# Attention and gated MLP on one core: transpositions in two tiles of 64 rows with split loads, the first pair's features written in place, and an order drawn anew

## The chip, the cores and the metric

The kernel runs on one core of a Trainium2 chip. The metric is the device time of one execution in microseconds; for the kernel before, the median of three runs is 740.95 us (740.59 to 742.3). Engines are named as in the profile: PE (TensorE matmul), PEld (its weight loads), DVE (VectorE), ACT (ScalarE), POOL (GpSimd) and SP, whose queue issues nearly all DMAs.

## What is computed

```python
# q, k, v: (4, 8, 768, 64); proj: (64, 6)
q_bits = einsum('bhsd,dk->bhsk', q, proj) > 0        # the same for k
mask = q_bucket[:, :, :, None] == k_bucket[:, :, None, :]
scores = where(mask, q @ k.T / 8, -1e9)
attn_out = softmax(scores) @ v                       # per batch and head
x = attn_out.transpose(0, 2, 1, 3).reshape(4, 768, 512)
h = gelu(x @ w_in); u, v = h[..., :512], h[..., 512:]
v_n = layernorm(v) * g_ln
v_s = einsum('ts,bsd->btd', w_sg, v_n) + b_sg[None, :, None]
out = x + (u * v_s) @ w_out
```

## The kernel before

The attention works on 16 pairs of heads (`NPAIR`), two heads side by side on the 128 partitions, 64 rows each. For each pair:

- `load` brings q and k in, one DMA per head and operand (4 per pair, all on SP's queue), as 128 token rows in partitions, 6 tiles of tokens, 2 x 64 columns. One buffer each holds q and k, so the next pair's load waits until the last reader of this pair's is done.
- `parts` transposes each with six 128x128 float32 transpositions (line L526; the identity streams, the data are the weights). ACT copies the result back into the same buffer (L536). `high` (ACT, L530) and `low` (DVE, L533) split it in a rounded part and a rest (`hq`, `lq`, `hk`, `lk`).
- `features` multiplies with the projection `pw`, 32 columns wide, four products side by side in four column tiles of the array (L553). `sign` (DVE, L556) makes bit features `fc` of it, and `scatter` sends them with four DMAs on SP's queue to their rows in `fq` and `fk` (L569). These were set to zero at the start by POOL (L486).
- `largest` ("M" below): for each of 6 tiles of queries and 2 halves of keys, four matmuls of 64 rows (two heads at once in two row tiles, feature product plus score product, L584) into two PSUM banks, and DVE takes the largest (L589, tile `mx`).
- `shift` spreads the maxima into a feature row (DVE L597, PE L602, ACT L608).
- `weigh` ("W"): for each of 12 tiles, eight matmuls of 64 rows (L624), ACT's exponential to `p` (L629), POOL's sums (L642).
- `weighted` ("AV"): the products with v (L654), for each half of the queries; the sums over keys (L678), and for the pair two ahead the feature products. `finish` sends the sums through DRAM and back as a reciprocal (SP: L695, L696, L699, L701; DVE: L697), scales the result on DVE (L703, `xt`) and stores it (L705).

PSUM has eight banks; an M and a W take two each. Maxima run four steps (`AHEAD`) ahead of the W that they belong to. Beside the attention the weights of the MLP are converted in jobs on DVE, POOL and ACT (L372 to L392). The MLP that follows (L845 hidden v, L876 hidden u, L894 gate, L923 output; four batches) streams dense matmuls; the first batch's hidden v starts inside the attention's end.

The order of all this is not the code's order. `Plan.add` takes for each step an engine, a cost and a priority; `Plan.order` runs a list scheduler over them and records instructions in that order, and each engine takes its own in order. The numbers at the top of the file (`HID`, `AVP`, `PREP`, `OM`, ...) are offsets of those priorities.

Of the kernel before, what the change touches and what calls it, by code (L numbers as in the profile page):

```python
# [21 lines left out]
MLP = {"xl": "POOL", "gm": "DVE", "gl": "POOL", "wg": 450.84, "wo": 131.34, "x": 480}  # L22
# [3 lines left out]
HID = 308.55  # L26
AVP = 3.07
S0P = -1.32
AHEAD = 4
PREP, SHIFTP, FINP, WSTEP, WP = 8.92, -3.65, 6.26, 37.69, 29.58  # L30
LOADS = "SP"
GPLACE = 4
XLATE = 7.75
FEAT = 2.17
LOWP = 7.32
LOADP = -0.4
LATF = 3.2
# [11 lines left out]
ADDW = 1  # L49


class Plan:
# [23 lines left out]
    def __init__(self):  # L76
        self.groups, self.tags = [], {}
# [21 lines left out]
    def add(self, engine, cost, prio, fn, r=(), w=(), dma=0, port=None, form=None, lat=0.0):  # L99

        port = engine == "POOL" if port is None else port
        g = {"e": engine, "c": cost, "p": prio, "fn": fn, "dma": dma, "n": len(self.groups), "slots": [], "port": port, "form": form, "lat": lat}
# [163 lines left out]
def kernel(  # L266
# [58 lines left out]
    frow = setup.tile([1, 2, P], F32, name="frow")  # L325
    nc.vector.memset(frow, 0.0)
    fv = frow.rearrange("a f (s b c) -> a f s b c", s=2, c=FB)
# [6 lines left out]
    nc.vector.memset(fv[:, 1, 1, :, MROW:MROW + 1], 1.0)  # L334
    pw = const.tile([P, 2, Q], F32, name="pw")
# [13 lines left out]
    fcol = const.tile([P, 2], F32, name="fcol")  # L349
# [88 lines left out]
    for i in range(2):  # L438
        nc.tensor.transpose(psb[:, 7, i:i + 1], frow[:, i, :], ident[:1, :1])
    nc.vector.tensor_copy(fcol, psb[:, 7, 0:2])  # L440
# [16 lines left out]
    if True:  # L457
# [27 lines left out]
        for t in ftiles[0] + ftiles[1]:  # L485
            nc.gpsimd.memset(t.bitcast(F32), 0.0)  # L486
# [15 lines left out]
        def load(n, prio):  # L502
# [3 lines left out]
            for s, (nm, src) in enumerate((("q", q), ("k", k))):  # L506
                t = early.ring([P, NT, 2, D], F32, nm, 1)
                for j in range(2):
                    def fn(eng, t=t, j=j, src=src):
                        eng.dma_start(t()[:, :, j, :], src[st.b, 2 * st.hp + j].rearrange("(t p) d -> p t d", t=NT))  # L510
                    dma(prio + 0.2 * s, 1.09, fn, w=[(t, j)], e=LOADS)
# [7 lines left out]
        def parts(st, s, prio):  # L519
# [3 lines left out]
            def tr():  # L523
                for hf in range(2):
                    for i in range(HT):
                        nc.tensor.transpose(tp()[:, hf, i * P:(i + 1) * P],  # L526
                                            raw()[:, hf * HT + i].rearrange("p j d -> p (j d)"), ident)
# [7 lines left out]
            plan.add(PE, 0.654, prio, tr, [raw], [tp])  # L535
            plan.add(ACT, 0.81, prio, lambda: nc.scalar.copy(x_of(raw).rearrange("p (a b) -> p a b", a=2), tp()[:, :, :SH]), [tp], [raw])  # L536
            def split(p1, p2):
                plan.add(ACT, 0.81, p1 + OH[s], high, [raw], [hh])
                plan.add(DVE, 0.98, p2 + OL[s], low, [raw, hh], [lo], port=True)
# [6 lines left out]
        def features(st, prio, merged=False):  # L546
# [13 lines left out]
            else:  # L560
                plan.add(PE, 0.66, prio, project, st.raw, [fp], form="col32")
            st.sign = lambda prio: plan.add(DVE, 0.56, prio, sign, [fp], [fc])
            st.fc = fc

# [8 lines left out]
        def largest(st, t, prio):  # L573
# [13 lines left out]
            for kh in range(2):  # L587
                plan.add(PE, 0.346, prio + 0.01 * kh + OM[2 * t + kh], lambda kh=kh: mm(kh), [*st.hi, *st.ft], [sc[kh]], form="row")
                plan.add(DVE, 0.95, prio + OM[2 * t + kh], lambda kh=kh: nc.vector.tensor_reduce(  # L589
                    mx()[:, i, :, kh], sc[kh]()[:, :, :SH], axis=AX.X, op=ALU.max, negate=True), [sc[kh]], [(mx, (kh, i))])  # L590

        def shift(st, hf, prio):
# [5 lines left out]
                m()[:, :, MROW::BL], mx(), axis=AX.X, op=ALU.min), [mx], [m])  # L598
# [5 lines left out]
            plan.add(PE, 0.18, prio, spread, [m], [tp])  # L604
# [381 lines left out]
```

## Time and profile before

| | us |
|---|---|
| median of 3 runs | 740.95 |
| the profiled execution's own time | 739.75 |
| its span, first to last instruction | 738.0 |
| PE busy in the span | 717.1 |
| DVE busy | 544.0 |
| POOL busy | 459.8 |
| ACT busy | 379.5 |

The span has a start (to about 30 us, when PE waits for loads and features), the attention (to 434 us), a passage in which the attention's last halves are finished beside the first batch's MLP, and from there to the end the MLP. Busy PE time counts overlapping and pipelined matmuls as one stretch; it tells where PE waits, and how fast it streams is read from start times.

### The profile page before, as it was taken

The page shows a single profiled execution, that of the slowest core. Times are in us where ns is not written, and L with a number is a line of the kernel's source. Part 1 is how long each engine was busy: PE and PEld are TensorE (multiplying, and loading weights), DVE is VectorE, ACT ScalarE, POOL GpSimd, SP SyncE. Part 2 cuts the span into 40 slices and gives each one's busy share as a digit, 9 for nine tenths or more (in the row PEclk, how much of TensorE's full clock was granted, in tenths as well). Part 3 has the DMA queues.
Part 4 walks back from the last instruction along what each step waited for, and adds up shares of the span by engine and source line. Part 5 has one row for each costly group of instructions (what it writes and reads, how often), then busy time and mean ns, then how long its engine had stood idle before and what let it go on. Part 6 is the DMA issues. An engine that isn't in the chain of part 4 may idle for free.

```text
span 738.0 us, 14443 instructions
## 1 busy us (share of the span) xinstructions
PE 717.1 (97%) x5300; PEld 566.5 (77%) x5300; DVE 544.0 (74%) x859; ACT 379.5 (51%) x623; POOL 459.8 (62%) x465
## 2 busy tenths in 40 slices
PE   6899999999999999999999999999999999999997
PEld 5676676666767666676766669998999889988996
DVE  3887899788898888878788878655864486347733
ACT  3565566665757656565765556530761066106510
POOL 2578889889887878778597976570463045404230
PEclk8999999999999999999999999999999999999999
DMA  6214543653675464255343235935220601061004
GB/s 139 70 45 103 127 114 90 154 132 94 155 143 123 93 149 108 70 128 125 96 108 95 73 85 135 239 68 139 34 64 23 157 15 43 1 147 25 1 1 115
DMA packets 180839, 70.59 MB, mean 96 GB/s; under 512 B 158112, under 2 KB 170528, under 8 KB 180768
## 3 DMA queue, kind: packets, MB, share of 16 engines
q1 hardware_dynamic: 180320, 69.01, 39.3%
q10 hardware_dynamic: 448, 0.66, 0.6%
q8 instruction: 42, 0.69, 0.4%
q14 instruction: 29, 0.24, 0.1%
HBM read 51.61 MB, written 17.24 MB: 93 GB/s over the span
## 4 chain that ended last, share of the span: by engine, by line
PE 76%; DMA 10%; DVE 9%; SPq 2%; issue 2%; ACT 1%; POOL 0%; DVEq 0%; ACTq 0%
PE psb L624 15%; PE psb L654 13%; PE psb L894 11%; PE psb L923 9%; PE psb L845 8%; PE psb L876 7%; PE psb L584 7%; DVE mx L589 4%; DMA r<-sq 2%; PE psb L526 2%; DMA rs<-r 2%; PE psb L678 1%; PE psb L553 1%; DMA sq<-s 1%; PE psb L602 1%
## 5 line engine op out<-in xcount | busy, mean ns | idle before, releaser
L642 POOL TENSOR_TENSOR sum<-sum,p 128x384 f32<-128x384 f32 x256 | 240.7, 977 | 54.8 <-ACT p L629 54.7
L589 DVE TENSOR_REDUCE mx<-psb 128x2 f32<-128x768 f32 x192 | 174.2, 950 | 39.7 <-PE psb L584 39.2
L629 ACT ACTIVATE p<-psb 128x768 f32<-128x768 f32 x192 | 147.1, 815 | 24.3 <-PE psb L624 20.8
L654 PE MATMUL psb<-p,v 128*64 128x385 f32 x768 | 131.2, 491 | 0.0
L654 PEld LDWEIGHTS psb<-p,v 128*64 128x64 f32 x768 | 52.3, 137 | 71.7 <-issue 62.4
L642 POOL TENSOR_TENSOR sum<-p,p 128x384 f32<-128x384 f32 x64 | 71.2, 1133 | 19.5 <-ACT p L629 19.5
L624 PE MATMUL psb<-hq,hk 64*128 64x384 f32 x384 | 72.0, 370 | 5.3 <-DVE mx L589 5.1
L584 PE MATMUL psb<-fk,fq 64*128 64x384 f32 x384 | 68.8, 353 | 2.3 <-DVE mx L589 2.3
L855 POOL TENSOR_TENSOR mv<-mv,epsr 128x1 f32<-128x1 f32 x24 | 13.8, 574 | 86.4 <-DVE mv L854 81.2
L584 PE MATMUL psb<-hk,hq 64*128 64x384 f32 x384 | 66.0, 339 | 0.0
L624 PE MATMUL psb<-lq,hk 64*128 64x384 f32 x384 | 64.9, 333 | 0.0
L624 PE MATMUL psb<-fq,fk 64*128 64x384 f32 x384 | 64.9, 332 | 0.0
L624 PE MATMUL psb<-hq,lk 64*128 64x384 f32 x384 | 64.8, 332 | 0.0
L894 PE MATMUL psb<-wgl,zh 128*128 128x384 f32 x192 | 64.2, 335 | 0.4 <-POOL wgl L817 0.4
L894 PE MATMUL psb<-wgh,zh 128*128 128x384 f32 x192 | 64.1, 334 | 0.0
L894 PE MATMUL psb<-wgh,zl 128*128 128x384 f32 x192 | 64.1, 334 | 0.0
L905 POOL TENSOR_TENSOR gs<-gt,gs 128x384 fp32r<-128x384 f32 x32 | 33.6, 1056 | 48.9 <-ACT gs L902 45.6
L669 ACT COPY un<-psb 128x385 f32<-128x385 f32 x32 | 15.4, 482 | 94.1 <-PE psb L654 94.1
L829 ACT ACTIVATE h<-psb 128x384 f32<-128x384 f32 (+1 forms) x56 | 29.4, 535 | 66.8 <-PE psb L845 59.9
L923 PE MATMUL psb<-woh,gs 128*128 128x512 f32 x192 | 59.9, 389 | 0.0
L897 DVE TENSOR_TENSOR gt<-psb,b_bc 128x384 f32<-128x384 f32 x32 | 17.8, 556 | 46.3 <-PE psb L894 43.5
L624 PEld LDWEIGHTS psb<-hq,hk 64*128 64x128 f32 x384 | 36.1, 184 | 16.8 <-DVE mx L589 11.3
(111 smaller groups left out, 1576.4 us busy)
## 6 DMA issues: line engine op xcount, KB each, us to landing
q<-in_q_dram SPq DMA_DIRECT2D x32, 192.0 KB, 4.3
k<-in_k_dram SPq DMA_DIRECT2D x32, 192.0 KB, 3.6
v<-in_v_dram SPq DMA_DIRECT2D x16, 384.0 KB
rs<-r SPq DMA_DIRECT2D x64, 96.0 KB, 3.0
xs<-xt SPq DMA_DIRECT2D x32, 192.0 KB, 3.3
x<-xs SPq DMA_DIRECT2D x16, 384.0 KB, 3.5
rx<-xs SPq DMA_DIRECT2D x96, 64.0 KB, 2.3
out_dram<-ob SPq DMA_DIRECT2D x24, 256.0 KB, 2.3
```

The source lines that it names most:

```text
L584: nc.tensor.matmul(sc[kh]()[:, j, :SH], x[0]()[row(j), qs], x[1]()[row(j), kh * SH:(kh + 1) * SH], start=(n == 0), stop=(n == 1))
L589: plan.add(DVE, 0.95, prio + OM[2 * t + kh], lambda kh=kh: nc.vector.tensor_reduce(mx()[:, i, :, kh], sc[kh]()[:, :, :SH], axis=AX.X, op=A ...
L624: nc.tensor.matmul(sc[i]()[:, j, :SH], x()[row(j), ks], y()[row(j), cs], start=(n == 0), stop=(n == 3))
L629: plan.add(ACT, 0.81, prio, lambda i=i: nc.scalar.activation(p[i]()[:, :, :SH], sc[i]()[:, :, :SH], AF.Exp), [sc[i]], [p[i], ticks[-1]])
L642: plan.add(POOL, 1.03, prio + 0.6, lambda i=i, j=j, first=first: nc.gpsimd.tensor_add(sums()[:, j], (first or sums)()[:, j, :SH], p[i]()[: ...
L654: nc.tensor.matmul(av()[row(j), :SH + 1], v_()[:, j, kt, :], p[kt]()[:, j, :], start=(kt == 0), stop=(kt == NT - 1))
L829: plan.add(ACT, ua - 0.02, prio, lambda: nc.scalar.activation(h2()[:, :n], ps()[:, :n], AF.Square), [ps], [h2])
L845: nc.tensor.matmul(ps(), x()[:, ts_], w[:, c, FH:FF], start=(c == 0 and n == 0), stop=(c == NC - 1 and n == 2))
L876: nc.tensor.matmul(ps()[:, :SH], w[:, c, fs], x()[:, cs], start=(c == 0 and n == 0), stop=(c == NC - 1 and n == 2))
L894: nc.tensor.matmul(vp()[:, :SH], z()[:, t, fs], w()[:, t, cs], start=(t == 0 and n == 0), stop=(t == NT - 1 and n == 2))
L905: nc.gpsimd if e == POOL else nc.vector).tensor_sub(gl()[:, cs], gt(), gh()[:, cs].bitcast(F32)),
L923: nc.tensor.matmul(po(), a()[:, ts_], w()[:, f, :], start=(f == 0 and n == 0), stop=(f == NF - 1 and n == 2))
```

## The change

1. **Transpositions.** For all pairs but the first, each load is split in two DMAs of 64 partitions: rows 0 to 63 hold tokens 0 to 383, rows 64 to 127 tokens 384 to 767. Each 128x128 transposition becomes two of 64 rows and 64 streamed columns, in the two row tiles of the array and into different PSUM banks. The matmuls M and W have the same two row tiles.
2. **First pair.** Its q and k keep the whole transpositions. Its features are made by `direct`: a projection `pwd` as wide as the array, whose columns lie where the features belong, for each operand and half of the tokens; DVE's sign writes straight into `fq` and `fk`. The four scatter DMAs and the zeroing of these two tiles fall away; PE has four full-width products in place of four side by side, DVE four signs in place of one. M now waits for the halves that it reads alone. One of the first pair's two k loads is issued by ACT's queue.
3. **Order.** The constants at the top are other numbers, and a table `SHAPE` adds an offset to the priority of each kind of step, cyclically by its count.

```diff
-MLP = {..., "wg": 450.84, "wo": 131.34, "x": 480}
+MLP = {..., "wg": 452.33, "wo": -53.82, "x": 459.7}
-HID = 308.55
+HID = 277.71
...
+SHAPE = {"A": [0.0, 0.0, 0.0, -1.0, ...], ..., "T": [0.03, 1.6], ...}
...
+        if tag in SHAPE:
+            i = self.count[tag] = self.count.get(tag, -1) + 1
+            prio += SHAPE[tag][i % len(SHAPE[tag])]
...
+    nc.vector.tensor_copy(pwd.rearrange("p s (i w) -> p s i w", w=FW)[:, :, :, 0], pw)
...
-        for t in ftiles[0] + ftiles[1]:
+        for t in ftiles[1]:
             nc.gpsimd.memset(t.bitcast(F32), 0.0)
...
+                    if not n:
...
+                        dma(prio + 0.2 * s, 1.09, fn, w=[(t, j)], e=ACT if s and j else LOADS)
+                    for r in range(2 if n else 0):
+                        def fn(eng, t=t, j=j, r=r, src=src):
+                            eng.dma_start(t()[row(r), :, j, :],
+                                          src[st.b, 2 * st.hp + j, r * SH:(r + 1) * SH].rearrange("(t c) d -> c t d", c=D))
+                        dma(prio + 0.2 * s, 0.55, fn, w=[(t, (j, r))], e=LOADS)
...
+                for t in range(NT):
+                    for r in range(2):
+                        nc.tensor.transpose(tp()[:, r, t * D:(t + 1) * D],
+                                            raw()[row(r), t].rearrange("p j d -> p (j d)"), ident[row(r), row(r)])
...
+        def direct(st, s, prio):
+            fp, ft = ps_two(), st.ft[s]
+            def project(hf):
+                nc.tensor.matmul(fp()[:, hf, :SH], pwd[:, s, :], x_of(st.raw[s])[:, hf * SH:(hf + 1) * SH], start=True, stop=True)
+            def sign(hf):
+                nc.vector.tensor_scalar(ft()[:, hf * SH:(hf + 1) * SH], fp()[:, hf, :SH], fcol[:, 2 + 2 * s:3 + 2 * s],
+                                        fcol[:, 3 + 2 * s:4 + 2 * s], op0=ALU.is_gt, op1=ALU.mult)
```

How the order moves is shown at three places. First PE at the third pair's transpositions, beside W (lines L624 before, L665 now) and M (L584 before, L625 now) of the pairs ahead. `hq`, `lq` and `fq` are parts and features of q, `ident` the identity. Before:

```order
L584 MATMUL psb<-fk_172,fq_171 128x384 x2
L584 MATMUL psb<-hk_0_343,hq_0_308 128x384 x2
L526 MATMUL psb<-ident,k_358 128x128 x6
L526 MATMUL psb<-ident,q_393 128x128 x6
L624 MATMUL psb<-hq_0_262,hk_0_273 128x384 x2
```

Now, on the same engine and for the same pair:

```order
L625 MATMUL psb<-hk_0_406,hq_0_364 128x384 x2
L553 MATMUL psb<-ident,q_422 128x64 x12
L665 MATMUL psb<-hq_0_271,hk_0_285 128x384 x2
L665 MATMUL psb<-hq_0_271,lk_0_303 128x384 x2
L665 MATMUL psb<-lq_0_282,hk_0_285 128x384 x2
L665 MATMUL psb<-fq_180,fk_181 128x384 x2
L625 MATMUL psb<-fk_183,fq_182 128x384 x2
L625 MATMUL psb<-hk_0_406,hq_0_364 128x384 x2
L553 MATMUL psb<-ident,k_485 128x64 x12
L665 MATMUL psb<-hq_0_271,hk_0_285 128x384 x2
```

One block of twelve full transpositions has become two blocks of twelve half ones, with a W and an M between them.

Second, PE at the start of the program (`frow` holds constants, `pw` and `pwd` the projection). Before:

```order
L526 MATMUL psb<-ident,q_249 128x128 x6
L526 MATMUL psb<-ident,k_252 128x128 x6
L553 MATMUL psb<-q_249,pw 32x384 x2
L553 MATMUL psb<-k_252,pw 32x384 x2
L526 MATMUL psb<-ident,q_285 128x128 x6
L584 MATMUL psb<-fk_170,fq_169 128x384 x2
```

Now:

```order
L548 MATMUL psb<-ident,q_258 128x128 x6
L596 MATMUL psb<-q_258,pwd 128x384
L548 MATMUL psb<-ident,k_261 128x128 x6
L596 MATMUL psb<-q_258,pwd 128x384
L596 MATMUL psb<-k_261,pwd 128x384 x2
L625 MATMUL psb<-fk_181,fq_180 128x384 x2
```

The second pair's q no longer stands ahead of the first M, and k's transpositions now stand behind the first half of q's projection.

Third, SP's queue where the thirteenth pair's q and k are loaded (`s`, `sq`, `r` and `xs` belong to `finish`). Before, the four loads:

```order
L510 DMA q_3695<-in_q_dram 128x6x64 x2
L510 DMA k_3721<-in_k_dram 128x6x64
L705 DMA xs_108<-xt_3719 128x384
L510 DMA k_3721<-in_k_dram 128x6x64
L696 DMA sq_3747<-s_0_213 128x6
```

Now:

```order
L736 DMA s_0_222<-sm_3827 4x192
L530 DMA q_3876<-in_q_dram 64x6x64 x3
L746 DMA xs_114<-xt_3892 128x384
L530 DMA q_3876<-in_q_dram 64x6x64
L530 DMA k_3920<-in_k_dram 64x6x64
L737 DMA sq_3928<-s_0_222 128x6
L530 DMA k_3920<-in_k_dram 64x6x64 x3
```

Eight issues stand where four stood, and the steps of `finish` stand among them.

## Rows read from the trace of the kernel before

**Rows 1.** Busy us by stretch: stretch, PE, PEld, DVE, ACT, POOL, then granted clock.
```profile
10.00:20.00 10.00, 6.39 (x36) 5.48 (x36) 5.39 (x7) 1.84 (x3) 0.00 (x0) 0.66 0.42 98
50.00:400.00 350.00, 342.53 (x3151) 239.99 (x3149) 300.79 (x422) 216.91 (x346) 286.54 (x293) 1.00 0.50 117
434.00:500.00 66.00, 64.87 (x342) 59.28 (x343) 46.36 (x85) 33.50 (x59) 41.06 (x33) 1.00 0.56 133
500.00:738.00 238.00, 234.25 (x1192) 213.57 (x1190) 135.72 (x249) 86.06 (x152) 75.14 (x68) 1.00 0.25 59
```

**Rows 2.** Waits, 30 to 434 us: waiting, waited for, total us, times, longest.
```profile
PE psb L624 <- DVE mx L589: 4.0, 7, 1.0
...
DVE mx L589 <- PE psb L584: 34.6, 56, 1.8
...
DVE xt L703 <- DMA rs<-r: 1.5, 2, 0.8
...
SPq L695 <- ACT sm L692: 31.1, 17, 4.1
```

**Rows 3.** Timeline of PE around one block of transpositions: start us, length us.
```profile
67.95 0.33 PE L584 MATMUL psb<-fk,fq 64*128 64x384 f32 x2
68.12 0.34 PE L584 MATMUL psb<-hk,hq 64*128 64x384 f32 x2
68.39 0.88 PE L526 MATMUL psb<-ident,k 128*128 128x128 f32 x6
69.10 0.82 PE L526 MATMUL psb<-ident,q 128*128 128x128 f32 x6
69.85 0.44 PE L624 MATMUL psb<-hq,hk 64*128 64x384 f32 x2
70.13 0.34 PE L624 MATMUL psb<-hq,lk 64*128 64x384 f32 x2
```

**Rows 4.** Groups by form: busy us, mean ns of one, idle before.
```profile
L526 PE MATMUL psb<-ident,q 128*128 128x128 f32 x96 | 14.0, 284 | 4.2 <-DMA q<-in_q_dram 3.6 <-DVE mx L589 0.6
...
L602 PE MATMUL psb<-identr,m 128*66 128x128 f32 x96 | 12.6, 240 | 0.0
...
L584 PEld LDWEIGHTS psb<-hk,hq 64*128 64x128 f32 x384 | 37.3, 189 | 0.0
...
L894 PEld LDWEIGHTS psb<-wgh,zl 128*128 128x128 f32 x192 | 36.0, 188 | 0.0
...
L526 PEld LDWEIGHTS psb<-ident,q 128*128 128x128 f32 x96 | 11.2, 145 | 5.2 <-DMA q<-in_q_dram 4.2 <-DVE mx L589 0.8
```

**Rows 5.** Chain that ended last: start us, us, what.
```profile
47.18 0.46 PE psb L678 x8
```

**Rows 6.** Timeline of the start: start us, length us, engine.
```profile
6.43 0.80 ACT L536 COPY q<-psb 128x768 f32<-128x768 f32 x1
6.75 0.85 PE L526 MATMUL psb<-ident,k 128*128 128x128 f32 x6 [0.35 <-DMA k<-in_k_dram]
8.94 0.52 PE L553 MATMUL psb<-q,pw 128*32 128x384 f32 x2 [1.34 <-ACT k L536]
9.26 0.52 PE L553 MATMUL psb<-q,pw 128*32 128x384 f32 x2
10.58 0.67 DVE L556 TENSOR_SCALAR fc<-psb,fcol 128x384 f32<-128x384 f32 x1
11.32 1.20 SPq L569 DMA_DIRECT2D fq<-fc  x2
14.81 0.69 PE L584 MATMUL psb<-fk,fq 64*128 64x384 f32 x2
15.87 5.28 DVE L589 TENSOR_REDUCE mx<-psb 128x2 f32<-128x768 f32 x6 [4.61 <-PE psb L584]
```

**Rows 7.** Issues of SP's queue by line: ns min/median/max.
```profile
L510 SPq DMA_DIRECT2D q<-in_q_dram x32: 368/532/2824, 0.7 to 368.7; - x32
...
L701 SPq DMA_DIRECT2D rs<-r x64: 444/547/1927, 63.0 to 451.5; - x64
```

More of the change, by code (lines that the diff above doesn't have):

```diff
@@ L19 @@
 DRAM = bass.MemoryType.DRAM
-MLP = {"xl": "POOL", "gm": "DVE", "gl": "POOL", "wg": 450.84, "wo": 131.34, "x": 480}
+MLP = {"xl": "POOL", "gm": "DVE", "gl": "POOL", "wg": 452.33, "wo": -53.82, "x": 459.7}
 NSUM = 3
 BANKED = False
-HID = 308.55
-AVP = 3.07
-S0P = -1.32
+HID = 277.71
+AVP = 2.95
+S0P = -1.92
 AHEAD = 4
-PREP, SHIFTP, FINP, WSTEP, WP = 8.92, -3.65, 6.26, 37.69, 29.58
+PREP, SHIFTP, FINP, WSTEP, WP = 8.63, -3.32, 2.62, 11.18, 30
 LOADS = "SP"
 GPLACE = 4
[L33 to L37, printed above, removed]
+XLATE = -0.13
+FIRST = -9.48
+FEAT = 4.51
+LOWP = 6.96
+LOADP = -3.53
+LATF = 2.6
 OM = [0.01, 0.27, 0.0, 2.44, 0.37, 0.0, -1.25, 0.68, 0.49, 1.13, -0.06, 0.0]
@@ L334 @@
     nc.vector.memset(fv[:, 1, 1, :, MROW:MROW + 1], 1.0)
+    for s in range(2):
+        for f in range(2):
+            nc.vector.tensor_copy(gv[:, s, f, :, :, 0], fv[:, f, s, :2])
+    pwd = const.tile([P, 2, P], F32, name="pwd")
+    nc.gpsimd.memset(pwd, 0.0)
     pw = const.tile([P, 2, Q], F32, name="pw")
@@ L523, in tr @@
             def tr():
[L524 to L527, printed above, removed]
+                if not st.n:
+                    for hf in range(2):
+                        for i in range(HT):
+                            nc.tensor.transpose(tp()[:, hf, i * P:(i + 1) * P],
+                                                raw()[:, hf * HT + i].rearrange("p j d -> p (j d)"), ident)
+                    return
+                for t in range(NT):
+                    for r in range(2):
+                        nc.tensor.transpose(tp()[:, r, t * D:(t + 1) * D],
+                                            raw()[row(r), t].rearrange("p j d -> p (j d)"), ident[row(r), row(r)])
             def high():
@@ L533, in low @@
                 nc.vector.scalar_tensor_tensor(lo(), x_of(raw), fac, hh().bitcast(F32), op0=ALU.mult, op1=ALU.subtract)
-            plan.add(PE, 0.654, prio, tr, [raw], [tp])
-            plan.add(ACT, 0.81, prio, lambda: nc.scalar.copy(x_of(raw).rearrange("p (a b) -> p a b", a=2), tp()[:, :, :SH]), [tp], [raw])
+            plan.add(PE, 0.35 if st.n else 0.66, prio, tr, [raw], [tp], form="row" if st.n else None, tag="T")
+            plan.add(ACT, 0.81, prio, lambda: nc.scalar.copy(x_of(raw).rearrange("p (a b) -> p a b", a=2), tp()[:, :, :SH]), [tp], [raw], tag="x")
             def split(p1, p2):
-                plan.add(ACT, 0.81, p1 + OH[s], high, [raw], [hh])
-                plan.add(DVE, 0.98, p2 + OL[s], low, [raw, hh], [lo], port=True)
+                plan.add(ACT, 0.81, p1 + OH[s], high, [raw], [hh], tag="hi")
+                plan.add(DVE, 0.98, p2 + OL[s], low, [raw, hh], [lo], port=True, tag="lo")
             st.split.append(split)
@@ L560, in features @@
             else:
[L561 to L562 removed]
+                plan.add(PE, 0.66, prio, project, st.raw, [fp], form="col32", tag="F")
+            st.sign = lambda prio: plan.add(DVE, 0.56, prio, sign, [fp], [fc], tag="sg")
             st.fc = fc
+        def direct(st, s, prio):
[5 more added lines that the diff above has]
+                                        fcol[:, 3 + 2 * s:4 + 2 * s], op0=ALU.is_gt, op1=ALU.mult)
+            for hf in range(2):
+                plan.add(PE, 0.66, prio + 0.01 * hf, lambda hf=hf: project(hf), [st.raw[s]], [(fp, hf)])
+                plan.add(DVE, 0.56, prio + 0.01 * hf, lambda hf=hf: sign(hf), [(fp, hf)], [(ft, ("f", hf))])
         def scatter(st, prio):
@@ L642, in weigh @@
                         plan.add(POOL, 1.03, prio + 0.6, lambda i=i, j=j, first=first: nc.gpsimd.tensor_add(
-                            sums()[:, j], (first or sums)()[:, j, :SH], p[i]()[:, j, :SH]), [p[i]] + ([first] if first else []), [(sums, j)])
+                            sums()[:, j], (first or sums)()[:, j, :SH], p[i]()[:, j, :SH]), [p[i]] + ([first] if first else []), [(sums, j)], tag="A")
         def weighted(st, hf, prio, owed, nxt=None):
@@ L723, in rest @@
         def rest(st, prio):
-            st.sign(prio + OF[0])
-            scatter(st, prio + OF[1])
+            if st.n:
+                st.sign(prio + OF[0])
+                scatter(st, prio + OF[1])
             for s, f in enumerate(st.split):
@@ L741 @@
             prepare(n, (-12, -3)[n])
-            features(sts[n], (-12, -3)[n] + 0.3)
+            if n:
+                features(sts[n], (-12, -3)[n] + 0.3)
+            else:
+                for s in range(2):
+                    direct(sts[n], s, FIRST + 0.1 * s)
             rest(sts[n], (-12, -3)[n] + 0.3)
```

48 lines of the change are left out of this document (25 added, 23 removed).

## The prediction

> **What bounds the kernel now.** I read the busy times by stretch first. From 50 to 400 us, the steady attention, PE is busy 342.5 of 350 us, DVE 300.8 (86%), POOL 286.5 (82%) [rows 1]. From 500 us on, the MLP, PE is busy 234 of 238 us and nothing else comes near; in the passage ahead of it 64.9 of 66. So PE is late nearly everywhere, and a microsecond of PE work taken out of the attention is worth up to a microsecond, while an order that only lets PE wait less has some 7.5 us to win in those 350.
>
> The waits come second. The longest of PE's own in the attention is W's for DVE's maxima, 4.0 us; against it DVE waits 34.6 us for M on PE [rows 2]. The two alternate, with PE ahead of DVE in need. DVE is next in line: its slack is about 14% of the time.
>
> Third, the timeline of PE around a block of transpositions. M's beats (one matmul in each of the two row tiles) start 0.17 us apart [rows 3]. The reader is to see what the block costs beyond its twelve transpositions: M's last beat starts at 68.12 and would be over for PE at 68.29; W's first starts at 69.85, and its second not 0.17 but 0.28 later. So the block takes 69.85 - 68.29 + 0.11 = 1.67 us out of PE's stream, some 0.05 of it a wait by my reading; I use 1.6. Twelve at their own pace are less: one lasts 273 ns and six 0.82 us [rows 3] (the group's mean is 284 [rows 4]), so they start (820 - 273) / 5 = 109 ns apart, 1.31 us for twelve. The other 0.3 us lies at the two edges, where PE goes from row tiles to the whole array and back.
>
> The start is a chain of its own: copy of q, transpositions and copy of k, feature products at 8.94, sign at 10.58, scatter DMAs issued from 11.32, M at 14.81, first maxima at 15.87 [rows 6]. PE stands idle in it, and from 10 to 20 us the granted clock is 0.66 on average, a stretch at the lower of its two levels (1.2 GHz) after idle time; DVE is busy 5.4 us of these 10 [rows 1].
>
> **Transpositions.** Removed: 12 full ones per pair in 15 pairs. Added: 24 of 64 rows and 64 columns, 12 beats if the two row tiles work at once as M's do. How long such a beat is no row shows. Below: half of 109, 55 ns, since half as many columns stream. Nearest: the short matmuls of L602, three of them 12.6 / 32 = 0.39 us and one 240 ns, so (394 - 240) / 2 = 77 ns apart, with weights of 66 columns [rows 4]. Above: 109 ns, if the weights are the limit and a beat's two loads come one after the other. A load for a full transposition takes 145 ns on average. M's take 189, which could mean that two row tiles share a path; but L894's loads of the whole array take 188 too [rows 4], so the 189 is not from sharing. I take 60 ns, nearer the lower end, since columns set the pace of full transpositions: 12 x 60 = 0.72 us per pair. The edges go, since M and W around have the same row tiles. Saved per pair 1.6 - 0.72 = 0.88 us. The second pair's lie in the start, under DVE; for the other 14, 12.3 us of PE work. Bounds: at 55 ns 13.2 us; at 109 ns 4.1 us; at 109 ns with an edge of 0.3 us at each of the two blocks that now stand apart, 4.3 us lost.
>
> A row limits the pace by instructions: eight matmuls of L678 took 0.46 us, 58 ns each [rows 5], and at that pace 24 would take 1.38 us per pair, no better than now but for the edges. That row streams 192 columns in four tiles, so I don't take it for a floor. The Trainium skill, "TensorE: Matmul & The Clock Gate", section "Wait — 56ns, not 53.3ns?", has a rule that speaks against this change: starts never come closer than about 25 ns, and with hardware decode off a sequencer spends about 62 ns on each matmul. By the first a beat of two could take 50 ns and the gain would stand; by the second 24 would take 1.49 us, an estimate from that page, and most of it would be gone. L678's 58 ns lies below the second figure, and no row shows which holds for a run of twelve.
>
> What is late next where PE gains is DVE. If 12.3 us come out, its share goes from 86 to about 89%. On average that fits into its 34.6 us of waiting for M [rows 2], but not at each place, and PE's wait for maxima will grow. I give a quarter back: 3.1 us, net **9.2 us**.
>
> **Split loads.** Per pair four more issues on SP; a load of 128 partitions takes it 532 ns, and one of 64 partitions (L701) 547 [rows 7], so a half is no cheaper: 4 x 0.53 = 2.1 us per pair, 32 us in all, beside the four scatter issues that fall away. Bytes and pieces (256 B) are the same. SP has idle time: one wait alone, for ACT's sums, holds it 31.1 us [rows 2]. So I cost it at nothing; without that cover it costs what the third rival says.
>
> **First pair.** Removed: the way from sign to M, 14.81 - 11.25 = 3.6 us, of which M now waits for none [rows 6]. Added on PE: a beat of the four column tiles takes 9.26 - 8.94 = 0.32 us and four products take two, so one full-width product 0.65 us, four 2.6 in place of 0.65; on DVE three more signs of 0.67, 2.0 us. With the new order: q is copied by 7.23, its first product 7.25 to 7.9, k's transpositions 0.85 to 8.75, q's second product to 9.4, k copied at about 9.6, k's products to 10.95, the last sign to about 11.7, DVE's `lk` to 12.7, then maxima, against 15.87 now. That is 3.2 us. M is fed earlier still, and DVE bounds this stretch. The k load on ACT's queue saves an issue of half a microsecond ahead of k's landing, but k's transpositions now wait for q's product: nothing. I take **3 us**; bounds 0 (the clock falls at a worse place, or W's first steps wait for the second pair's transpositions, which stand ahead of them) and 4.5.
>
> **Order.** The redrawn order keeps the shape: two halves per pair, AV, then W and M mixed. M and W now alternate one to one around the transpositions instead of two to two, which feeds DVE more evenly. What it can win is bounded by PE's idle 7.5 us, and it can lose as much. I take 0, bounds -5 and +5. The MLP streams as before: 0. In the passage PE idles 1.1 us of 66 [rows 1]; what is issued there moves with the attention's end: 0, bounds -1 and +2.
>
> **Sum**, against the profiled execution's own 739.75 us (span 738.0): 739.75 - 9.2 - 3 = 727.5. The median of the runs is 1.2 above that execution: 728.7, and I write 728.
>
> **The rivals.**
> - *The half transpositions don't pair up.* Beats of 109 ns, from weights or from instructions. For it: L678's 58 ns per matmul. Against it: M's pairs do run together, and the weight loads look independent of tiling. Then 4.1 us less a quarter, 3.1, and the start's 3: 734.8. (The page's 62 ns per matmul would end here as well.)
> - *DVE takes the bound.* PE gains, but at each M DVE is late instead, since all maxima must pass through it, six in 5.28 us [rows 6], 0.88 each. For it: 86%. Against it: 34.6 us in which it waits for M. Then a quarter of the gain stays: 741 - 3 - 3 = 735.
> - *SP delays `finish`, and the time grows.* SP takes its steps in order; four more issues per pair stand among the steps of `finish`, DVE reaches `xt` before its reciprocal has landed, the maxima queued behind `xt` on DVE wait, and M, W and AV on PE behind them. Now `xt` waits 1.5 us in all [rows 2]. Each pair in which the issues come through costs up to 2.1 us; it decides from 6 of 14 pairs on, where 12.6 us exceed the forecast's gain. At 7 pairs 741 - 12.2 + 14.7 = 743. Against it: SP's waits.
> - *The order wins more than PE's idle now shows*, since waits at the start and in the passage go too: 741 - 12.2 - 8 = 721 and, at the lower bounds of the other terms, 716.
>
> **How the numbers follow.** Forecast, 722 to 733: 0.58. First rival 0.13, second 0.09, third 0.11, fourth 0.09. The range reaches over the first two rivals with a spread of 3 us and over part of the fourth: 718 to 738. About 0.2% (1.5 us) is what a measurement of this kernel can tell from no change. Faster than 739.5: the forecast, the fourth, and nearly all of the first two, 0.86. The same: the edge of these and of the third, 0.05. Slower: 0.09.
>
> **What would show it.** In the profile of the changed kernel: half transpositions in pairs that start 55 to 65 ns apart, and no longer gap to the next W (step one right); 110 ns or more between pairs, or a first W beat that is 0.1 us late (wrong). First maxima at about 12.7 us and the first W some 3 us ahead of now. PE's share from 50 us to the end of the attention still over 97% (DVE did not take the bound), DVE's near 89%. `xt`'s wait for its DMA under 3 us (the third rival out). The MLP's length the same to within 1 us. The forecast would be wrong if the attention's steady stretch got shorter by less than 5 or more than 15 us.

## The result: slower by 1.1%, where 1.7% faster was forecast

| | before | changed |
|---|---|---|
| median of six runs each on one chip, us | 741.63 (740.59 to 744.14) | 750.35 (745.07 to 751.16) |
| the profiled execution's own time | 739.75 | 746.71 |
| its span | 738.0 | 744.9 |

The ratio is 1.0111 [1.0091, 1.0132]. The forecast was 728 us, with a range to 738. The profiled execution of the changed kernel is a quick one, 3.6 us under the median of its kernel. So the trace tells where time went, and the ratios tell how much.

### The profile page after: what moved, and what is told of

Read it like the earlier page. It is cut to its first block, busy times and chain, and to the rows that moved or that the text cites. A ratio compares the mean times of both kernels' runs of the same rounds, so it can differ in the third digit from the quotient of the medians.

```text
span 744.9 us, 14945 instructions
## 1 busy us (share of the span) xinstructions
PE 714.7 (96%) x5484; PEld 564.1 (76%) x5484; DVE 550.4 (74%) x867; ACT 378.7 (51%) x623; POOL 459.6 (62%) x464
## 5 line engine op out<-in xcount | busy, mean ns | idle before, releaser
L683 POOL TENSOR_TENSOR sum<-sum,p 128x384 f32<-128x384 f32 x256 | 243.9, 981 | 65.2 <-ACT p L670 61.4
L670 ACT ACTIVATE p<-psb 128x768 f32<-128x768 f32 x192 | 149.5, 814 | 43.7 <-PE psb L665 34.6
L625 PE MATMUL psb<-fk,fq 64*128 64x384 f32 x384 | 71.2, 363 | 15.6 <-DVE mx L630 11.0
L683 POOL TENSOR_TENSOR sum<-p,p 128x384 f32<-128x384 f32 x64 | 74.1, 1178 | 19.1 <-ACT p L670 19.1
L665 PE MATMUL psb<-hq,hk 64*128 64x384 f32 x384 | 73.8, 376 | 3.8 <-DVE mx L630 3.3
L625 PE MATMUL psb<-hk,hq 64*128 64x384 f32 x384 | 67.1, 340 | 0.0
L665 PE MATMUL psb<-lq,hk 64*128 64x384 f32 x384 | 66.3, 336 | 0.0
L665 PE MATMUL psb<-fq,fk 64*128 64x384 f32 x384 | 66.2, 336 | 0.0
L665 PE MATMUL psb<-hq,lk 64*128 64x384 f32 x384 | 66.1, 336 | 0.0
L625 PEld LDWEIGHTS psb<-fk,fq 64*128 64x128 f32 x384 | 37.6, 187 | 27.7 <-DVE mx L630 16.0
```

Source lines behind the costliest of these rows:

```text
L625: nc.tensor.matmul(sc[kh]()[:, j, :SH], x[0]()[row(j), qs], x[1]()[row(j), kh * SH:(kh + 1) * SH], start=(n == 0), stop=(n == 1))
L665: nc.tensor.matmul(sc[i]()[:, j, :SH], x()[row(j), ks], y()[row(j), cs], start=(n == 0), stop=(n == 3))
L670: plan.add(ACT, 0.81, prio, lambda i=i: nc.scalar.activation(p[i]()[:, :, :SH], sc[i]()[:, :, :SH], AF.Exp), [sc[i]], [p[i], ticks[-1]], t ...
L683: plan.add(POOL, 1.03, prio + 0.6, lambda i=i, j=j, first=first: nc.gpsimd.tensor_add(sums()[:, j], (first or sums)()[:, j, :SH], p[i]()[: ...
```

## The profile after

Busy time by stretch, as in [rows 1] (stretch, PE, PEld, DVE, ACT, POOL, then the granted clock):

```profile
10.00:20.00 10.00, 8.00 (x57) 4.55 (x58) 9.64 (x13) 2.37 (x3) 0.00 (x0) 0.93 0.35 79
50.00:400.00 350.00, 331.85 (x3245) 233.92 (x3242) 296.66 (x409) 213.86 (x342) 283.88 (x289) 0.99 0.46 114
500.00:744.90 244.90, 241.20 (x1224) 219.69 (x1222) 140.22 (x257) 87.72 (x156) 78.94 (x72) 1.00 0.24 58
```

In the steady attention PE now idles 18.2 us of 350, where it idled 7.5. The MLP still streams; it begins later, as the attention's last product with v starts at 435.3 us in place of 429.9. Here are the two parts that went nearly as forecast. First PE around one half block, as in [rows 3] (start us, length us):

```profile
39.25 0.34 PE L625 MATMUL psb<-hk,hq 64*128 64x384 f32 x2
39.43 0.53 PE L553 MATMUL psb<-ident,q 64*128 64x64 f32 x12
39.77 0.43 PE L665 MATMUL psb<-hq,hk 64*128 64x384 f32 x2
40.02 0.34 PE L665 MATMUL psb<-hq,lk 64*128 64x384 f32 x2
```

Twelve half transpositions begin 0.18 us behind M's last beat, so the way in has no edge, and W's first beat starts 0.34 us later. On the way out W's second beat comes 0.25 us behind its first, where 0.17 is the pace and 0.28 stood in [rows 3]: some 0.08 us of this edge stays. Counted as in the prediction a block takes 0.43 us out of PE's stream and a pair's two 0.85, in place of 1.67. Single start times in the blocks put the beats 62 ns apart. Second the start, as in [rows 6]:

```profile
7.45 0.91 PE L596 MATMUL psb<-q,pwd 128*128 128x384 f32 x2 [0.89 <-ACT q L563]
10.85 1.32 DVE L599 TENSOR_SCALAR fk<-psb,fcol 128x384 fp32r<-128x384 f32 x2 [0.32 <-PE psb L596]
11.58 0.45 PE L625 MATMUL psb<-fk,fq 64*128 64x384 f32 x2
12.96 6.13 DVE L630 TENSOR_REDUCE mx<-psb 128x2 f32<-128x768 f32 x7
```

M begins at 11.58 in place of 14.81, the maxima at 12.96 in place of 15.87, and the first W (from the start times) at 21.89 in place of 24.85. What went wrong stands in the waits from 30 us to 440 (waiting, waited for, total us, times, longest), as in [rows 2]:

```profile
PE psb L625 <- DVE mx L630: 9.4, 7, 2.1
PE psb L625 <- DMA fk<-fc: 4.2, 4, 1.9
PE psb L665 <- DVE mx L630: 3.3, 6, 1.4
...
DVE mx L630 <- PE psb L625: 40.9, 45, 3.3
DVE wy L395 <- DMA w<-in_moe_w_in_dram: 9.5, 8, 3.1
...
SPq L736 <- ACT sm L733: 15.2, 10, 5.1
```

PE's waits for DVE are longer than in [rows 2], and DVE's for PE are longer too. Two engines that both wait more for each other point to a third thing, and the rows name two candidates: weight loads `w` that have not landed when DVE reaches them, and scatters `fk` that have not landed when M wants them (not in the view before). The same wait for `w` in the kernel before, and then in the changed kernel with whole loads, which comes below:

```profile
DVE wy L381 <- DMA w<-in_moe_w_in_dram: 5.5, 3, 2.4
...
DVE wy L395 <- DMA w<-in_moe_w_in_dram: 2.5, 3, 1.4
```

The scatters' wait stays at 3.1 us with whole loads, so most of it belongs to the new order. SP's wait for ACT's sums, the cover in the prediction, has shrunk from 31.1 us to 15.2. `xt` does not wait at all.

One place shows the chain. Timeline of SP's queue in the changed kernel (start us, length of the issues):

```profile
238.05 0.69 SPq L530 DMA_DIRECT2D k<-in_k_dram  x1
238.83 1.30 SPq L530 DMA_DIRECT2D q<-in_q_dram  x2
240.22 0.56 SPq L746 DMA_DIRECT2D xs<-xt  x1
240.84 0.60 SPq L530 DMA_DIRECT2D q<-in_q_dram  x1
241.53 0.57 SPq L737 DMA_DIRECT2D sq<-s  x1
242.15 0.60 SPq L530 DMA_DIRECT2D q<-in_q_dram  x1
242.80 1.97 SPq L530 DMA_DIRECT2D k<-in_k_dram  x3
244.81 2.00 SPq L815 DMA_DIRECT2D wgd<-in_moe_w_sg_dram  x3
...
248.67 0.81 SPq L386 DMA_DIRECT2D w<-in_moe_w_in_dram  x1
```

And what DVE and PE did with it:

```profile
252.83 0.30 DVE L395 TENSOR_SCALAR wy<-w 128x256 int32<-128x256 int32 x1 [3.11 <-DMA w<-in_moe_w_in_dram]
253.03 0.95 DVE L630 TENSOR_REDUCE mx<-psb 128x2 f32<-128x768 f32 x1
...
254.04 0.69 PE L625 MATMUL psb<-fk,fq 64*128 64x384 f32 x2 [2.08 <-DVE mx L630]
```

The eight half loads and the issues among them stand back to back. The buffer of `w` came free at 247.34, when DVE's last reader ended, but SP reached that load only at 248.67. DVE, in order, stood 3.11 us at `wy` with a maximum queued behind it, and PE 2.08 us for that maximum's PSUM banks. SP's lateness is 1.33 of the 3.11 us; the rest comes from the 4.16 us that lie between the load's issue and DVE's start. In the kernel before SP reached the same load in time, and DVE waited there too, but less, and PE's wait for maxima in that half is 0.3 us:

```profile
248.50 0.30 DVE L381 TENSOR_SCALAR wy<-w 128x256 int32<-128x256 int32 x1 [2.06 <-DMA w<-in_moe_w_in_dram]
```

The next views say what a stop of PE can cost beside its own length:

```profile
251.90:254.00 2.10, 0.07 (x2) 0.00 (x0) 1.17 (x3) 1.14 (x2) 1.06 (x2) 1.00 0.51 153
254.10:257.40 3.30, 3.30 (x28) 3.21 (x30) 2.45 (x4) 1.00 (x2) 3.30 (x4) 0.50 0.02 1
```

After 2 us without work PE's granted clock is 0.50, the lower level (1.2 GHz), for 3.4 us. The same happens at 134.6, after a stop of 1.8 us; there DVE waits for no load, but is busy with other steps without a break. Not every such stop is followed by it: two others in this execution, 1.7 us at 201.5 and 1.9 at 399.2, were not. In the attention of the kernel before the clock did not fall.

## Experiments

Each ratio is to the kernel before on the same chip, whose medians there were 740 to 741.6 us; 0.1% is 0.74 us. Line numbers are those of the kernel that was edited, unless said.

**Parts of the change, one at a time.** The order of before with half transpositions and split loads in all pairs:

```diff
+                        for r in range(2):
+                            eng.dma_start(t()[row(r), :, j, :], src[..., r * SH:(r + 1) * SH].rearrange("(t c) d -> c t d", c=D))
...
+                        nc.tensor.transpose(tp()[:, r, t * D:(t + 1) * D], raw()[row(r), t]..., ident[row(r), row(r)])
```

> The order of the kernel before, step for step, with half transpositions and split loads for all pairs in their places. If the redrawn order is what costs time, the saved PE work (0.85 us per pair by the trace of after: beats of 62 ns and no edges) shows here: 741.6 less 9 to 13, about 730. If the doubled issues on SP's queue are what costs, it is eaten here too: 742 to 750.

Measured: 761.31 us, 1.0274 [1.0244, 1.0304]. The order of before with whole transpositions, and each load only cut in two DMAs of 64 partitions:

```diff
+                        for r in range(2):
+                            eng.dma_start(t()[row(r), :, j, :], src[...].rearrange("(t p) d -> p t d", t=NT)[row(r)])
```

> The order of the kernel before and its whole transpositions, each load split in two of 64 partitions issued back to back. If the redrawn order costs the time: the same as before within 2 us, 740 to 744. If the issues on SP cost it: 64 more issues of 0.53 us come through in part, 750 to 756.

Measured: 764.86 us, 1.0309 [1.0278, 1.0341]. Both times lie above the dearer of their two ranges. Cutting the loads in two, 64 more issues and nothing else, costs 23 us in the order of before; in the redrawn order it costs 9.3, as shown below. DVE's waits from 30 to 434 us in this run:

```profile
DVE wy L381 <- DMA w<-in_moe_w_in_dram: 12.5, 6, 3.5
DVE sq L699 <- DMA sq<-s: 8.7, 8, 2.3
DVE xt L705 <- DMA rs<-r: 7.4, 5, 2.4
```

Three carriers, of which the prediction named the last. The changed kernel's order and first pair, with whole loads and whole transpositions throughout:

```diff
-                if not st.n:
+                if True:
...
+                            if r == 0:
+                                eng.dma_start(t()[:, :, j, :], src[...].rearrange("(t p) d -> p t d", t=NT))
```

> The order of the changed kernel with its first pair, but whole transpositions and whole loads (the first half's step issues the whole load, the second's nothing). If the redrawn order costs: still slower than the kernel before, and slower than the changed one by the transpositions' PE time as far as PE is late: 752 to 762. If the issues cost: back near the kernel before, 738 to 744.

Measured: 749.42 us, 1.0097 [1.0072, 1.0122], between the two ranges: with whole transpositions this order does harm of its own. Its blocks of whole transpositions stand apart, so each pair pays four edges in place of two; from the start times blocks and edges take 31.2 us after the first pairs, 28.2 before. And PE waits 3.7 us for the scatter of `fk`, which it does not before.

**Half transpositions without split loads.** The order of before, whole loads as before; row tile r transposes its 64 rows into bank r, and ACT's copy puts the runs of 64 columns in order:

```diff
+                        nc.tensor.transpose(tp()[:, r, t * D:(t + 1) * D], raw()[row(r), t]..., ident[row(r), row(r)])
...
-nc.scalar.copy(x_of(raw).rearrange("p (a b) -> p a b", a=2), tp()[:, :, :SH])
+nc.scalar.copy(x_of(raw).rearrange("p (t r c) -> p r t c", r=2, c=D), tp()[:, :, :SH].rearrange("p r (t c) -> p r t c", c=D))
```

> The kernel before in its own order, with whole loads as before and half transpositions in two tiles of 64 rows (row tile r writes bank r; ACT's copy puts the runs of 64 columns in order). Nothing else is changed, so this is the step on the transpositions by itself. If PE's gain of the block (0.88 us a pair, of which I gave a quarter back) reaches the end when SP has nothing more to issue: 730 to 735. If DVE takes nearly all of it: 739 to 742. If the copy with its runs is dearer on ACT (over 1 us in place of 0.8), ACT's sums come late and it is 742 to 746.

Measured: 738.49 us, 0.9967 [0.9944, 0.9989]. This lies between the first range and the second. In its trace blocks and edges take 17.9 us in place of 28.2, 10.3 less; 2.4 us (0.8 to 4.1 by the interval) reach the end. The changed kernel with the same two edits, so whole loads, half transpositions, its own order and first pair:

> The changed kernel in its own order and with its first pair, but with whole loads in all pairs; the half transpositions stay (their copy on ACT puts the runs in order). Theory A (split loads are the cost, the drawn order and the first pair are not): 726 to 734. Rival C (the drawn order costs some 8 us by itself, as the run with whole loads and whole transpositions suggested, 749.4 us): 738 to 744, which is that run less 6 to 11 us for the block and its edges.

Measured: 740.06 us, 0.9985 [0.9959, 1.0011], in rival C's range, and as it has it: the run before less 6 to 11 us. Counted from the order of before, three numbers add up: half transpositions in the order of before -0.33%, the new order with the first pair +0.18% (by the intervals -0.17 to +0.53, so not told apart from zero), the split loads 1.0111 against 0.9985, +1.26% or 9.3 us (7 to 12). The first two are not independent: in the new order, with whole loads, half transpositions win 1.12%, 8.3 us (0.9985 against 1.0097; 6 to 11), where blocks and edges go from 31.2 us to 17.9. How far the n-th product with v starts behind (or ahead of) that of before, in single executions, shows where:

| n | before, us | changed | split loads only | half transpositions only | changed, whole loads |
|---|---|---|---|---|---|
| 0 | 34.4 | -1.2 | +3.7 | -0.7 | -0.9 |
| 3 | 75.4 | -5.0 | +3.9 | -1.6 | -4.7 |
| 8 | 138.2 | +1.2 | +4.7 | -2.0 | -2.9 |
| 17 | 255.9 | +4.9 | +15.1 | -2.3 | -2.3 |
| 31 | 429.9 | +5.4 | +17.7 | -4.4 | -4.3 |

The changed kernel is 5 us ahead at 70 us, and loses 10 by 261 us, in the stretch in which weight jobs and `wgd` loads stand in SP's queue too. The same version with whole loads keeps most of its lead. Against it the changed kernel loses 9.7 us by the last row; 2.2 of them fall between n = 7 and 8 and 2.8 between 16 and 17, where the two stretches at the lower clock lie. The SP queue of that version at the same place (start us, length):

```profile
233.59 0.67 SPq L531 DMA_DIRECT2D k<-in_k_dram  x1
234.35 0.82 SPq L531 DMA_DIRECT2D q<-in_q_dram  x1
235.27 0.58 SPq L746 DMA_DIRECT2D xs<-xt  x1
235.90 0.42 SPq L531 DMA_DIRECT2D q<-in_q_dram  x1
236.42 0.70 SPq L737 DMA_DIRECT2D sq<-s  x1
237.18 0.43 SPq L531 DMA_DIRECT2D k<-in_k_dram  x1
237.65 2.21 SPq L815 DMA_DIRECT2D wgd<-in_moe_w_sg_dram  x3
...
243.31 0.35 SPq L386 DMA_DIRECT2D w<-in_moe_w_in_dram  x1
```

The rows and their order are the same but for the four extra loads. Here SP stands at `w` until its buffer is free, at 243.24, and DVE waits for it 1.39 us in place of 3.11:

```profile
246.68 0.30 DVE L395 TENSOR_SCALAR wy<-w 128x256 int32<-128x256 int32 x1 [1.39 <-DMA w<-in_moe_w_in_dram]
```

**Issues or transfers?** Second halves issued by ACT's queue, in the changed kernel and in the order of before:

```diff
-                            eng.dma_start(t()[row(r), :, j, :],
+                            (nc.scalar if r else eng).dma_start(t()[row(r), :, j, :],
```

> The changed kernel, with the second half of every load issued by ACT's queue at the same place of the order. If SP's issues hold up the weight loads and scatters: 735 to 742. If the order costs whatever the queue: 747 to 753.

> The kernel before in its own order, with half transpositions and split loads in all pairs (as in the first experiment, 761.3 us), but the second half of each split load is issued by ACT's queue. SP then has as many issues as before the change. Theory A (SP's issues are the cost): the 23 us of the split loads go, less some waits on ACT, whose queue is in order too; half transpositions then gain 4 to 9 us: 733 to 742, and DVE's waits for w loads from 30 us on fall from 12.5 to under 6 us. Rival B (the split transfers themselves are slow or come late, whoever issues them): 755 to 762.

Measured: 745.66 us, 1.0049 [1.0028, 1.007], and 758.06 us, 1.0219 [1.018, 1.0259]. The first lies between its two ranges, the second in rival B's. DVE's wait for `w` falls to 1.5 us in the one and from 12.5 to 3.8 in the other, as theory A has it, but only 0.62 and 0.55% are won, 4 to 5 us, the second hardly clear of the noise. PE's waits in the second, from 30 to 434 us, show part of the reason:

```profile
PE psb L586 <- DVE mx L591: 7.1, 7, 2.4
PE psb L626 <- ACT p L631: 4.4, 5, 2.0
PE psb L586 <- ACT p L631: 4.2, 5, 2.2
```

ACT's queue is in order too: its exponentials stand behind the issues, and PE behind the exponentials. Part of the cost moved with the issue; these two runs do not rule out rival B. The kernel before, with 64 extra DMAs of 1 KB on SP that nobody reads:

```diff
+                        eng.dma_start(extra[:, 4 * st.n + 2 * s + j, :], src[st.b, 2 * st.hp + j, 0:D, 0:EX])
```

> The kernel before, unchanged but for one small DMA more behind each load of q and k on SP's queue: 64 rows of 16 bytes into a buffer that nobody reads, 64 in all, 1 KB each. It adds SP's issue time and next to no bytes. Theory A (time of issue on SP): +15 to +25 us, 756 to 767. Rival B (the transfers of split loads): under +5 us, 741 to 746.

Measured: 752.38 us, 1.0157 [1.0131, 1.0183]. Issues with next to no bytes cost 12 us, which lies between the two theories and is about half of what the split loads cost in that order; DVE's waits for w, rs and sq are 11.0, 7.1 and 6.9 us. Last, the changed kernel with second halves cut to 64 rows of 16 bytes, and with them left out:

```diff
+                            if r:
+                                eng.dma_start(t()[row(r), 0, j, 0:4], src[..., SH:SH + D, 0:4])
```

> The changed kernel with the same issues on SP in the same order, but each second half load fetches only 64 rows of 16 bytes (1 KB in place of 96 KB), from the second pair on; the rest of its half is left out. If SP's time of issue is the cost, nothing is won by having no bytes: 747 to 752. If the transfers of the split loads are the cost, or compete with the others': 738 to 744.

> The changed kernel without the second half loads from the second pair on: 60 issues of SP and 5.8 MB left out, all else the same. If the 60 issues are the cost of the split loads: 736 to 742, as with whole loads (740.1). If it is not the issues but, say, when a half may start or where it stands in SP's order: 745 to 751.

Measured: 744.6 us, 1.0063 [1.0035, 1.0092], just outside the second range, and 739.01 us, 0.9979 [0.9958, 0.9999], as expected of issues. Of the split loads' 1.32% (the changed kernel against the last) 0.84% are the issues and 0.48% the bytes. The intervals leave the first number between 4 and 9 us and the second between 1 and 6; whole loads, which bring all the bytes, cost no more than none (0.9985 against 0.9979). Why bytes in halves should cost when bytes in whole loads do not stays open. SP's issues in the run with tiny halves, by line (ns min/median/max; the first the tiny ones of 1 KB, the second those of 96 KB):

```profile
L531 SPq DMA_DIRECT2D q<-in_q_dram x30: 465/614/717, 11.1 to 382.0; - x30
...
L533 SPq DMA_DIRECT2D q<-in_q_dram x30: 602/625/782, 10.3 to 381.3; - x30
```

An issue of 1 KB takes SP as long as one of 96 KB, and the median of a whole load of 192 KB in [rows 7], 532 ns, is no higher.

**Fewer issues, tried elsewhere.** `finish` loads `rs` in two DMAs of 64 rows, which broadcast one row each. One DMA of 128 rows saves 32 issues:

```diff
-eng.dma_start(rs()[row(j)], rd[j].partition_broadcast(D))
+None if j else eng.dma_start(rs(), rd.unsqueeze(1).to_broadcast([2, D, SH]))
```

> The kernel before, with the same merged load of `rs` and nothing else: 32 issues fewer on SP. Theory A says how much SP's queue costs the kernel before already: DVE waits there 5.5 us for w, 3.3 for sq and 1.5 for rs, so 734 to 738. If SP's idle time covered its issues before the change, as the prediction had it: 739 to 742.

> The changed kernel, with one issue on SP taken away per half: `finish` loads its reciprocals `rs` for both heads in one DMA (128 rows) in place of two of 64 rows; 32 issues of 0.55 to 0.6 us fall away, the bytes stay. Split loads and half transpositions stay. Theory A (the time of issues on SP is the cost; the split loads added 60 of them, worth about 9.5 us): a third to a half of it comes back, 743 to 747, and DVE's waits for w loads from 30 us on fall from 9.5 to under 6 us. Rival B (the split transfers themselves): within 2 us of the changed kernel, 748 to 752.

> The run with the order of before, whole loads and half transpositions (738.5 us), with the merged load of `rs`. There the block of transpositions saved PE 10.3 us in the trace, of which 6.5 were given back where PE goes between W and M and waits for maxima or exps. Theory A (they were given back because DVE, in order, is held by late DMAs): 731 to 736. Rival D (DVE's own work takes them back): within 2 us of that run, 737 to 740.

> The run with the changed kernel's order and first pair, whole loads and half transpositions (740.1 us), with the merged load of `rs`. Theory A: 733 to 738. Rival D (the drawn order and DVE's work bound it): 738 to 741.

Measured: 761.56 us, 1.0289 [1.0256, 1.0323]; 769.52, 1.0383 [1.034, 1.0426]; 755.04, 1.0191 [1.016, 1.0222]; 760.45, 1.0259 [1.0237, 1.0282]. All four miss both expectations; each is 17 to 21 us above the same version without the edit. So they say nothing for or against the issues: the merged DMA itself is slow. Timeline of the kernel before with that edit:

```profile
172.43 0.55 SPq L701 DMA_DIRECT2D rs<-r  x1
...
178.64 0.83 DVE L703 SCALAR_TENSOR_TENSOR xt<-un,rs 128x384 f32<-128x384 f32 x1 [3.42 <-DMA rs<-r]
```

`xt` starts 6.2 us after the issue, and 6.1 to 7.2 in the seven other places where it waits for `rs`. Of the kernel before the view of the tile `rs` says:

```profile
DMA to landing us min/median/max: 2.7/3.0/3.8
```

The runs do weigh the other half of the chain: DMAs that land 3 us later in front of a step in DVE's queue cost 17 to 21 us here, though DVE's waits for `rs` in that run are 12.2 us from 30 to 434 us.

**Why the half transpositions give so little.** Three of DVE's seven steps left out of each weight job (in the order of before, with whole and with half transpositions; all loads stay):

```diff
-        vec(lambda: V.tensor_single_scalar(y(), x(), -0x800000, op=ALU.bitwise_and), [x], [y], True)
-        vec(lambda: sts(yf(), lo().bitcast(U32), 2.0 ** -52, yf(), op0=ALU.mult, op1=ALU.mult), [w, y], [y])
-        vec(lambda: V.tensor_add(xf(), xf(), yf()), [x, y], [x])
```

> The kernel before with three of DVE's eight steps left out of each weight job (the low part of the 64-bit weights; 2.15 us a job, 51 us of DVE's time in the attention); the loads, the waits for them and the order stay. With whole transpositions PE is the bound in most halves, so DVE's work should cost little: 735 to 740. It is the base for the next run.

> The order of before, whole loads and half transpositions, with the same three steps of DVE left out. Theory D (in the halves with transpositions DVE, in order, is full, and takes PE's gain back): the half transpositions now gain 7 to 10 us against the run before this one, not 2.5: 726 to 731. Rival (the gain is lost elsewhere, on ACT, POOL or the buffers): 2 to 4 us, 732 to 737.

Measured: 739.01 us, 0.9979 [0.9963, 0.9996], and 734.71 us, 0.991 [0.9894, 0.9926]. With a lighter DVE half transpositions win 0.69%, 5.1 us, twice as much as without. That is more than the rival expected and less than theory D did; the time itself lies in the rival's range, and the 0.36% by which the gain grew are only just clear of their error, 0.32. So a full DVE is part of it, and not shown to be all. Two stretches of the run with half transpositions alone, each one half of a pair with a block of transpositions in it, and then the same two halves of the kernel before:

```profile
213.90:228.00 14.10, 13.46 (x145) 9.26 (x141) 13.72 (x18) 9.95 (x16) 12.77 (x15) 1.00 0.51 106
239.50:253.60 14.10, 13.58 (x143) 9.31 (x139) 11.89 (x18) 9.74 (x16) 11.71 (x13) 1.00 0.36 72
...
216.20:230.30 14.10, 13.85 (x131) 9.65 (x127) 12.90 (x18) 9.98 (x16) 12.78 (x14) 1.00 0.59 110
241.80:255.90 14.10, 13.85 (x131) 9.64 (x127) 11.91 (x18) 9.86 (x16) 11.72 (x13) 1.00 0.34 71
```

In the first DVE now works 13.72 of 14.10 us. In the second it works 11.89 and waits 2.1 at `wy` for `w`, as it did before. Both halves took 14.1 us before as well: PE got its block done sooner, by 0.66 us, and its waits for DVE's maxima grew from 0.2 and 0.3 us to 0.6 and 0.5, which is part of what was given back. They are not all alike: of 13 halves with a block between 61 and 399 us (from the start times) eight became shorter, by 0.4 to 1.8 us, two stayed and three became longer. So I gave the `w` loads a second buffer, in this version and in the changed kernel, so that SP need not stand at such a load until DVE has read the last one:

```diff
-            return early.ring(shape, dt, tag)
+            return early.ring(shape, dt, tag, 2 if tag == "w64" else 1)
```

> The order of before, whole loads and half transpositions, with two buffers in place of one for the weight loads `w`: SP no longer stands at such a load until DVE has read the last one. The planner puts some weight steps elsewhere for that. If late w loads in DVE's queue are what takes the rest of PE's gain: 731 to 736, and DVE's waits for w near 0. If not: 737 to 740.

> The changed kernel with two buffers for `w`. If the split loads do their harm through late w loads (DVE waits 9.5 us for them from 30 us on): 742 to 746. If through all of `finish` and the scatter alike, or through transfers: 747 to 751.

Measured: 734.71 us, 0.9931 [0.9914, 0.9948], and 743.1 us, 1.0034 [1.001, 1.0057], both in the range for late loads of `w`: 2.7 and 5.7 us less than without it (0.6 to 4.8 and 3.4 to 8.0). DVE's wait for w is gone in the first and 1.2 us in the second. The first, with whole loads, is the best of the full kernels here and 1.8% below the change. It is not the buffer alone: the planner put some DVE and SP steps elsewhere for it.

## Why the prediction failed, point by point

Forecast were 12.2 us less; measured were 8.2 more (1.11%). Of the 20.4 us between, 9.3 are the split loads. The other 11.1 are that transpositions, first pair and order together, with whole loads, gave 0.15%, 1.1 us (-0.8 to 3.0), where 12.2 stood. So two steps failed: the split loads at nothing, and the quarter given back. Of the 11.1 us the sums can't say how much belongs to that quarter and how much to the order at 0, since half transpositions win 2.4 us in one order and 8.3 in the other.

- *Split loads at nothing: this step failed.* It has the wrong sign of the result by itself, 9.3 us where 0 stood. The count of issues was right, and their price nearly: a half load's median is 0.62 us (in the changed kernel too) where 0.53 stood, so four more cost 2.5 us a pair and not 2.1. Of what the split loads cost, 6.2 us (4 to 9) are the issues, by the runs with tiny halves and without them; why the bytes should cost the rest stays open. The error was to set 31.1 us of waiting by SP, summed over 404 us, as cover against issues that stand in one row of eight. SP's wait [rows 2] lies in front of steps whose turn has come; behind a row of loads SP has no wait, and what stands there is late by the length of the row. No upper bound went into the range either.
- *The third rival* had the mechanism (SP late, DVE in order, PE behind) and too small a chance. Its place was wrong: it watched `xt`, and named `xt`'s wait under 3 us as the sign that it is out. `xt` did not wait at all. The redrawn order had spared it (8.6 us in the order of before, in the first run above), and the weight loads carried the delay.
- *Transpositions.* Pace right: 62 ns against 60, two blocks of 0.34 us against 0.72 in all. Of the edges 0.08 us a block stays, so a pair saves 0.81 us where 0.88 stood. The rival that they don't pair up is out. L678's 58 ns, which spoke for it, were misread: by their start times four of the eight start within 0.02 us and the other four 0.19 us later, and the 0.46 us hold the length of the last. By the Trainium skill, "TensorE: Matmul & The Clock Gate", section "Wait — 56ns, not 53.3ns?", a sequencer spends about 62 ns on each matmul with hardware decode off; here a pair starts every 62 ns, 31 ns for each, so that limit did not hold. What failed is the quarter given back: this step was mis-sized. In the order of before 10.3 us were saved and 2.4 came through, so some three quarters were given back; in the new order, with whole loads, 13.3 were saved and 8.3 came through, so some four tenths. A full DVE takes part of it, and late loads of `w` as far as the runs with two buffers tell; where the rest goes stays open.
- *DVE takes the bound* is right in part, and had too small a chance. The 86% were a mean; [rows 1] could not show it, but stretches of one half each would have: between 61 and 399 us of the kernel before they go from 75 to 95%.
- *First pair:* 2.9 us at the first maxima and 3.0 at the first W, as forecast. That it reaches the end was not tested by itself.
- *Order at 0:* with whole loads and half transpositions, order and first pair together cost 0.18%, 1.3 us (-1.3 to 3.9). If the first pair's 3 us hold to the end, the order costs some 4, within the bounds given; with whole transpositions the two together cost 0.97%, 7.2 us, of which the edges of blocks that stand apart are 3.0, and by this count the order is beyond its bound. One place is in the trace: PE waits for scatters (3.1 us in the run with whole loads), of which [rows 2] has none.
- *Signs named in advance:* PE's share over 97% in the steady attention, measured 94.8%; DVE's near 89%, measured 84.8%. Both said that neither engine was the bound, as the waits then showed. The MLP was to stay the same to within 1 us: from the attention's last product with v to the end it is 309.6 us, 308.1 before.

## What to carry to other kernels

A queue that issues in order has no idle time to give away in general: look at the place where the new issues stand, at what comes behind them in the same queue, and at which in-order engine reads that. When one more DMA is issued, its price on that queue is the issue, 0.5 to 0.6 us here for 1 KB as for 96, so a load cut in two should pay for itself on the engine that bounds that very place; here half transpositions were to be had with whole loads and another pattern in a copy. Measure an engine's share in stretches as short as the pattern repeats, since a mean of 86% had halves of 95% in it.

## What was not expected of the hardware

- A broadcast of two rows to 64 partitions each took some 6.2 us, from its issue to the start of the step that waited for it, in one DMA of 192 KB, where two of 96 KB took 2.7 to 3.8 each to land. The Trainium skill, "DMA: Bandwidth & Descriptors", section "Why a DMA increments its semaphore by 16 and not by 1", says that a DMA is spread over the largest number of engines, up to 16, that divides the slowest dimension (of those larger than 1) of both its patterns. The merged source has a slowest dimension of 2. The 6.2 us agree with that; no run here shows the number of engines.
- Cutting the bytes of a DMA from 96 KB to 1 KB leaves its time on SP's queue as it was, 614 against 625 ns.
- A stop of PE of 1.8 us and one of 2.1 in the steady attention of the changed kernel were each followed by 3.4 us at the lower clock; stops of 1.7 and 1.9 us in the same execution were not, nor was the one of 1.8 us in the kernel before.
